# Attention with logits and ranks in PSUM, two chunks' routing interleaved, weight loads behind the chunks, last ranks ahead of the gathered rows

## The chip, the cores and the metric

The kernel runs on one core of one Trainium2 chip, as one launch. The metric is device time in microseconds (us), the median of three runs. The engines are named as in the profile: PE is TensorE (matrix products), PEld its loading of the stationary operand, DVE VectorE, ACT ScalarE, POOL GpSimd, SP SyncE, which only issues transfers. L525 is line 525 of the kernel whose profile or instruction list is shown. PSUM is the accumulator memory behind PE, eight banks of 512 fp32 numbers per partition; SBUF is the on-chip memory of the other operands.

## The reference

Three parts follow each other on 3072 tokens of width 512: a linear attention with a decaying state, a mixture of experts of which each token takes one, and a gated block.

```python
# attention: 4 batches, 8 heads, 768 tokens, head size 64
for t in range(S):
    state = gamma * state + einsum('bhd,bhe->bhde', k[:, :, t], v[:, :, t])
    y[:, :, t] = scale * einsum('bhd,bhde->bhe', q[:, :, t], state)
# mixture: 8 experts, 512 -> 1024 -> 512
logits = x @ w_gate;  e_idx = argmax(logits, axis=1)
gate_w = softmax(logits)[arange(N), e_idx];  eom = sigmoid(x @ w_output_gate)
for e in range(E):
    mask = e_idx == e
    out[mask] = gate_w[mask] * eom[mask, e] * (relu(x[mask] @ w1[e]) @ w2[e])
# gated block: rms norm, two products 512 -> 1536, silu(g) * val, product back to 512
```

## The kernel before

The attention works through 24 chunks of 128 tokens (4 batches of 6). For chunk n PE makes the products of keys and queries (`qk`, L492), which DVE masks by decay (`am`, L499), then in PSUM bank 4 the sum of queries times state (QS, L515, not in the first chunk of a batch, n = 0, 6, 12, 18) and of masked scores times values (PV, L520). DVE scales this sum by `rs` (one slab for each of the six positions in a batch) into `xt` (L525). The state is updated by the product ST (L538) and copied from PSUM to SBUF, half by ACT (L542) and half by DVE (L543). The products of xt with the identity and both gate matrices (`rows`, L549) give in PSUM banks 5 and 6 the token rows and 16 logits in four parts each; DVE adds the parts into `lg` (L554), ACT copies the rows (L557).

Routing of a chunk: a chain of small DVE operations on 128x8 numbers (L564 to L571) finds the largest logit, the expert as a one-hot vector `ohb`, a running count `run_cnt`, and the gate's argument; ACT takes two exponentials (L570, L574). `place` then lets PE count the rank of each token inside its expert (L580 to L582), DVE makes weight and list position (L583 to L590), ACT scales the row and stores it to `xr` (L613, L617), and POOL scatters the token's number into a list in DRAM (L604).

Behind the chunks expert 0 starts on the first 448 tokens of its list. Tokens from older chunks are gathered from `xr` by POOL (L280) and turned by PE (`settle_in`, L629); tokens of the last `NDIRECT` chunks are brought in by a product with a 0/1 matrix `pt` (`direct_in`, L620) of the row's rounded part `rh` and its remainder `rl`. `split` divides the sum in PSUM into two operands, and the expert's products follow (L310, L323).

The expert weights (64 tiles of 128x1024) are loaded by SP (`loads_to`) and split in two by ACT (L179) and POOL (L180) (`convs_to`); the first `NPRE` of them beside the chunks, one tile at every odd n from 3 on. The order of each engine's instructions is the order of the code: in one pass of the loop `load(n+3)`, `vscale(n+1)`, `qk(n+1)`, `rows(n-1)`, `qs_pv(n)`, `st_up(n)`, `place(n-1)`, then weights. A tracker of tiles adds the waits between engines; PSUM is one tile with eight banks for it, and it orders accesses of two engines to the same bank.

Of the kernel before, what the change touches and what calls it, by code (L numbers as in the profile page):

```python
# [103 lines left out]
def fused_kernel(  # L104
# [336 lines left out]
    with ExitStack() as es:  # L441
# [86 lines left out]
        def st_up(n):  # L528
# [13 lines left out]
            ACT.activation(out=s[0:64, :, 0:64], in_=v[0:64], func=AF.Copy)  # L542
            DVE.tensor_copy(out=s[64:128, :, 64:128], in_=v[64:128])  # L543

        def rows(n):
# [14 lines left out]
            sc = tp.tile([128, 12], F32, name="sc", tag="sc")  # L560
            col = [sc[:, i:i + 1] for i in range(12)]
            mx, pm, nmx, sm, nz, ez, s1, t1, gw, pos = col[:10]
            ohb = tp.tile([128, NE], BF16, name="ohb", tag="ohb")
            DVE.tensor_reduce(out=mx, in_=lg[:, 0:8], axis=AX.X, op=ALU.max)  # L564
            DVE.scalar_tensor_tensor(out=junk[:, 0], in0=lg[:, 0:8], scalar=mx, in1=prio, op0=ALU.is_ge, op1=ALU.mult)
            DVE.tensor_scalar(out=nmx, in0=mx, scalar1=-1.0, scalar2=None, op0=ALU.mult)
            DVE.tensor_reduce(out=pm, in_=junk[:, 0], axis=AX.X, op=ALU.max)
            DVE.tensor_scalar(out=ohb, in0=prio, scalar1=pm, scalar2=None, op0=ALU.is_equal)
            DVE.tensor_tensor(out=run_cnt[:, n + 1], in0=run_cnt[:, n], in1=ohb, op=ALU.add)
            ACT.activation(out=junk[:, 1], in_=lg[:, 0:8], func=AF.Exp, bias=nmx, accum_out=sm)  # L570
            DVE.scalar_tensor_tensor(  # L571
                out=junk[:, 2], in0=lg[:, 8:16], scalar=-1.0, in1=ohb, op0=ALU.mult, op1=ALU.mult, accum_out=nz
            )
# [526 lines left out]
```

## Time and profile before

| | us |
|---|---|
| median of three runs (range) | 1115.93 (1115.77 to 1116.07) |
| profiled execution, its own time | 1114.17 |
| its span | 1112.2 |
| PE busy in the span | 1054.8 (95%) |
| DVE busy | 545.0 (49%) |
| ACT busy | 382.3 (34%) |
| POOL busy | 336.0 (30%) |

The span runs from the first to the last recorded instruction; the profiled execution's own time is 2.0 us longer. PE is busy for 95% of the span, but not evenly: in the page's 40 slices of 27.8 us its busy tenths are 7, 7, 8, 8, 7, 8 and then 9 almost to the end. The first five slices hold the chunks, and there DVE stands at 4, 6, 9, 9 and 9 tenths. The chunks end at about 151 us and the first product of expert 0 begins at 171.47 us.

### The profile page before, as it was taken

Reading aid. Unit: us, or ns where it says so; the run is one execution under the profiler, and the core shown is the slowest. Engines: PE = TensorE matmul, PEld = TensorE weight load, DVE = VectorE, ACT = ScalarE, POOL = GpSimd, SP = SyncE. Lnnn points to the kernel's source line nnn. Section 1 sums busy time; section 2 is a strip of 40 time slices with the busy share of each in tenths; the row PEclk is TensorE's granted clock in tenths of the full one; section 3 lists DMA queues with packets and bytes.
Section 4 is the critical chain, followed back from the end, with each engine's and each line's share of the span. In section 5 each row is a group of like instructions: output and inputs, shape, how many; then the busy total and the mean of one; then the engine's idle time right before and its main releaser. Section 6 shows DMA issues by size and latency. Waiting matters only on the chain.

```text
span 1112.2 us, 16373 instructions
## 1 busy us (share of the span) xinstructions
PE 1054.8 (95%) x6393; PEld 985.4 (89%) x6394; DVE 545.0 (49%) x1045; ACT 382.3 (34%) x721; POOL 336.0 (30%) x271
## 2 busy tenths in 40 slices
PE   7788789999999999989899999999999999999995
PEld 6777769989999999988788999999999999999995
DVE  4699953256665676898888731111311122311111
ACT  1344433444444544565555431111311112211111
POOL 3355534556566656432433310000110000200002
PEclk9899989999999999999999999999999999999998
DMA  8999724446446555443343230000200000100001
GB/s 303 254 295 268 213 63 140 124 129 207 153 137 207 183 156 172 155 108 94 111 141 114 86 95 19 1 1 1 85 29 1 1 1 29 57 1 1 1 1 60
DMA packets 47864, 116.74 MB, mean 105 GB/s; under 512 B 12966, under 2 KB 24486, under 8 KB 44962
## 3 DMA queue, kind: packets, MB, share of 16 engines
q1 hardware_dynamic: 39602, 97.05, 28.9%
q0 software_dynamic: 4864, 12.53, 3.2%
q10 hardware_dynamic: 3312, 6.03, 1.5%
q8 instruction: 52, 0.85, 0.3%
q14 instruction: 34, 0.28, 0.1%
HBM read 93.06 MB, written 23.11 MB: 104 GB/s over the span
## 4 chain that ended last, share of the span: by engine, by line
issue 42%; PE 26%; DVE 8%; ACT 4%; POOL 4%; DMA 2%; POOLq 0%; DVEq 0%; ACTq 0%
PE ps L310 12%; PE ps L323 12%; DVE fb L203 2%; POOL out_dram L805 2%; POOL w L180 1%; DVE fb L200 1%; PE ps L296 1%; ACT fu L191 1%; DMA out_dram<-ob,perm 1%; DVE a L780 1%; ACT w L179 1%; DVE fu L206 1%; DVE fb L194 1%; PE ps L629 1%; ACT fu L192 1%
## 5 line engine op out<-in xcount | busy, mean ns | idle before, releaser
L772 PE MATMUL ps<-zh,w 128*128 128x384 f32 x960 | 257.5, 339 | 6.1 <-ACT a L779 6.1
L780 DVE TENSOR_TENSOR a<-a,ps 128x384 f32<-128x384 f32 x96 | 53.0, 552 | 322.7 <-PE ps L772 314.6
L772 PEld LDWEIGHTS ps<-zh,w 128*128 128x128 f32 x960 | 176.6, 190 | 10.9 <-ACT a L779 8.7
L180 POOL TENSOR_TENSOR w<-raw,w 128x1024 fp32r<-128x1024 f32 x64 | 154.7, 2428 | 102.6 <-ACT w L179 101.9
L772 PE MATMUL ps<-zl,w 128*128 128x384 f32 x480 | 162.4, 338 | 0.0
L772 PE MATMUL ps<-xh,w 128*128 128x384 f32 x576 | 154.5, 339 | 4.0 <-DVE a L780 2.6
L310 PE MATMUL ps<-xh,w 128*128 128x448 f32 (+7 forms) x512 | 149.6, 353 | 0.1
L790 PE MATMUL ps<-w,ah 128*128 128x512 f32 x564 | 145.3, 392 | 0.2 <-ACT ys L345 0.2
L805 POOL DMA_INDIRECT out_dram<-xw,perm x10 | 9.9, 992 | 420.9 <-ACT xw L803 417.9
L781 ACT ACTIVATE ah<-a 128x384 fp32r<-128x384 f32 x94 | 49.4, 525 | 203.7 <-DVE a L780 203.7
L790 PEld LDWEIGHTS ps<-w,ah 128*128 128x128 f32 x564 | 104.7, 188 | 16.5 <-ACT ys L345 0.6
L779 ACT ACTIVATE a<-ps 128x384 f32<-128x384 f32 x96 | 46.7, 487 | 200.8 <-PE ps L772 200.8
L772 PEld LDWEIGHTS ps<-xh,w 128*128 128x128 f32 x576 | 104.9, 188 | 7.1 <-DVE a L780 3.3
L323 PE MATMUL ps<-hh,w 128*128 128x448 f32 (+7 forms) x512 | 106.6, 350 | 0.0
L310 PEld LDWEIGHTS ps<-xh,w 128*128 128x128 f32 x512 | 95.2, 188 | 3.5
L772 PE MATMUL ps<-xl,w 128*128 128x384 f32 x288 | 96.9, 337 | 0.0
L323 PEld LDWEIGHTS ps<-hh,w 128*128 128x128 f32 x512 | 93.8, 188 | 2.9
L772 PEld LDWEIGHTS ps<-zl,w 128*128 128x128 f32 x480 | 91.0, 190 | 2.1
L310 PE MATMUL ps<-xl,w 128*128 128x448 f32 (+7 forms) x256 | 89.9, 351 | 0.0
L180 POOL TENSOR_TENSOR w<-fu,w 128x512 fp32r<-128x512 f32 x36 | 54.1, 1504 | 113.3 <-ACT w L179 113.3
L790 PE MATMUL ps<-w,al 128*128 128x512 f32 x282 | 80.1, 392 | 0.0
L782 DVE TENSOR_TENSOR al<-a,ah 128x384 fp32r<-128x384 f32 x94 | 52.5, 559 | 55.6 <-ACT ah L781 55.6
(154 smaller groups left out, 1490.5 us busy)
## 6 DMA issues: line engine op xcount, KB each, us to landing
raw<-wmoe SPq DMA_DIRECT2D x64, 512.0 KB
qkv<-att SPq DMA_DIRECT2D x22, 1024.0 KB
raw<-wm SPq DMA_DIRECT2D x36, 512.0 KB
xw<-z SPq DMA_DIRECT2D x8, 768.0 KB
xr<-row ACTq DMA_DIRECT2D x23, 256.0 KB
z<-ys SPq DMA_DIRECT2D x2, 912.0 KB
z<-ys SPq DMA_DIRECT2D x2, 896.0 KB
z<-ys SPq DMA_DIRECT2D x2, 864.0 KB
```

Source lines behind the costliest of these rows:

```text
L179: ACT.activation(out=dst[:, 0, c], in_=src, func=AF.Copy)
L180: POOL.tensor_tensor(out=dst[:, 1, c], in0=src, in1=f32(dst[:, 0, c]), op=ALU.subtract)
L203: lambda: DVE.scalar_tensor_tensor(out=b, in0=hi, scalar=-(1 << 30), in1=b, op0=ALU.bitwise_and, op1=ALU.bitwise_or),
L310: PE.matmul(p, lhsT=wtile[:, s, k * 128:(k + 1) * 128], rhs=x[w % len(xh)][:, k, 0:n], start=(i == 0), stop=(i == 3 * KB - 1),)
L323: PE.matmul(ps[:, 4 + k, 0:n], lhsT=wtile[:, s, 512 + k * 128:512 + (k + 1) * 128], rhs=h, start=(f == 0 and j == 0), stop=(f == NF - 1 an ...
L772: PE.matmul(ps[:, part, 0:BT], lhsT=w2(f, part, s, k * 128, (k + 1) * 128), rhs=zz[:, k], start=(i == 0), stop=(i == 3 * KB - 1),)
L779: ACT.activation(out=a, in_=ps[:, 0, 0:BT], func=AF.Silu)
L780: DVE.tensor_tensor(out=a, in0=a, in1=ps[:, 1, 0:BT], op=ALU.mult)
L781: ACT.activation(out=ah, in_=a, func=AF.Copy)
L782: DVE.tensor_tensor(out=al, in0=a, in1=f32(ah), op=ALU.subtract)
L790: PE.matmul(ps[:, o_bank[b % 2][t]], lhsT=x[:, t * 128:(t + 1) * 128], rhs=w2(f, 2, s, 0, 512), start=(f == 0 and j == 0), stop=(f == NF2 ...
L805: ins = POOL.indirect_dma_start(out=out[:, :], out_offset=bass.IndirectOffsetOnAxis(ap=pm[:, t0 + t], axis=0), in_=o, in_offset=None, boun ...
```

## The change

Logits: `lg` is no tile in SBUF any more but sixteen columns of PSUM bank 5, beside the rows. The gate matrices are negated once, so that the chain looks for the smallest logit and the negation `nmx` goes. Ranks: they add up in PSUM bank 7 over all chunks, with the products of `ohb` by `rest` (one minus the triangular matrix `uh`) and by `uh`; `run_cnt` goes. Routing: `choose(n-1)` (finding the expert) and `weigh(n-2)` (weight and position) are written as lists and issued one from each in turn; the rank of chunk n-2 stands between PV and ST of chunk n, and `place(n-2)` holds scatter, scaling and store.

State: ACT copies it whole; it is 64 wide rather than 128 with zeros, so QS is eight products with 64 partitions and 64 columns of the stationary operand instead of four with 128. The slabs rs[1] to rs[5] (256 KB each) are no longer loaded but made by ACT from rs[0], four operations in each of the passes n = 0 to 4. Weights: four tiles are asked for in passes 20 to 23, two converted in the loop and two behind it; expert 0's own pass converts the following ones at 1.5 a step from four on, where before it began at eight. `NDIRECT` is 4 instead of 3, so the list is read back after the scatter of chunk 19, and the gather is issued at n = 23 and not at n = 22. The order behind the loop is new.

```diff
-NPRE = 8
+NPRE = 6
...
-NDIRECT = 3
+NDIRECT = 4
...
+        ranks = ps[:, 7, 0:8]
+        lg = ps[:, 5, 320:336]
...
-                    PE.matmul(
-                        o[:, a], lhsT=st_sb[n % 2][:, a], rhs=qT[:, a], start=(a == 0), stop=True, skip_group_check=True
-                    )
+                    for r in (0, 64):
+                        PE.matmul(
+                            o[r:r + 64, a], lhsT=st_sb[n % 2][r:r + 64, a], rhs=qT[r:r + 64, a],
+                            start=(a == 0), stop=True, skip_group_check=True,
+                        )
...
-            ACT.activation(out=s[0:64, :, 0:64], in_=v[0:64], func=AF.Copy)
-            DVE.tensor_copy(out=s[64:128, :, 64:128], in_=v[64:128])
+            ACT.activation(out=s, in_=v, func=AF.Copy)
...
-            lg = tp.tile([128, 16], F32, name="lg", tag="lg")
...
+        def rank(n):
+
+            if n:
+                PE.matmul(ranks, lhsT=rest, rhs=rt[n - 1][2], start=False, stop=True, skip_group_check=True)
+            else:
+                PE.matmul(ranks, lhsT=oh[0:1], rhs=e3[0:1], start=True, stop=True, skip_group_check=True)
+            PE.matmul(ranks, lhsT=uh, rhs=rt[n][2], start=False, stop=True, skip_group_check=True)
...
+            nm, pm, sm, nz, ez = [sc[:, i:i + 1] for i in range(5)]
+
+            def chosen():
+                DVE.tensor_scalar(out=ohb, in0=prio, scalar1=pm, scalar2=None, op0=ALU.is_equal)
+                ACT.activation(out=junk[:, 1], in_=lg[:, 0:8], func=AF.Exp, scale=-1.0, bias=nm, accum_out=sm)
+
+            def gate():
+                DVE.scalar_tensor_tensor(
+                    out=junk[:, 2], in0=lg[:, 8:16], scalar=1.0, in1=ohb, op0=ALU.mult, op1=ALU.mult, accum_out=nz
+                )
+                ACT.activation(out=ez, in_=nz, func=AF.Exp)
...
+                lambda: DVE.tensor_reduce(out=nm, in_=lg[:, 0:8], axis=AX.X, op=ALU.min),
+                lambda: DVE.scalar_tensor_tensor(
+                    out=junk[:, 0], in0=lg[:, 0:8], scalar=nm, in1=prio, op0=ALU.is_le, op1=ALU.mult
+                ),
...
+            ii = tp.tile([128, 1], I32, name="ii", tag="ii", bufs=3)
+            rt[n] = (lg, sc, ohb, gw, pos, ii)
+            return [
+                lambda: DVE.tensor_scalar(out=s1, in0=sm, scalar1=1e-9, scalar2=None, op0=ALU.add),
+                lambda: DVE.scalar_tensor_tensor(
+                    out=junk[:, 3], in0=ranks, scalar=1.0, in1=ohb, op0=ALU.mult, op1=ALU.mult, accum_out=pos
+                ),
+                lambda: DVE.tensor_scalar(out=t1, in0=ez, scalar1=1.0, scalar2=s1, op0=ALU.add, op1=ALU.mult),
+                lambda: DVE.tensor_copy(out=ii, in_=pos),
+                lambda: DVE.reciprocal(out=gw, in_=t1),
...
+        def in_turn(*lists):
+            for i in range(max(len(x) for x in lists)):
+                for x in lists:
+                    if i < len(x):
+                        x[i]()
...
-            rk = ps[:, 7, (n % 2) * 8:(n % 2) * 8 + 8]
-            PE.matmul(rk, lhsT=oh[0:1], rhs=e3[0:1], start=True, stop=False)
-            PE.matmul(rk, lhsT=oh, rhs=run_cnt[:, n], start=False, stop=False)
-            PE.matmul(rk, lhsT=uh, rhs=ohb, start=False, stop=True)
...
-            if 2 <= n + 2 < CPB:
-                SP.dma_start(out=rs[:, n + 2], in_=rsc[:, n + 2])
...
-            if n == NCH - 2:
+            if n == NCH - 1:
                 ex.gather(0, CAPS[0], NT - NDIRECT * CH)
             qk(n + 1)
             if n >= 1:
                 rows(n - 1)
             qs_pv(n)
+            if n >= 2:
+                rank(n - 2)
             st_up(n)
-            if 1 <= n < NCH - 1:
-                place(n - 1)
-            if n == NCH - 3:
+            if n + 1 < CPB:
+                for a in range(NP):
+                    g = A_GROW + n * NP + a
+                    ACT.activation(out=rs[:, n + 1, a], in_=rs[:, 0, a], func=AF.Copy, scale=ca[:, g:g + 1])
+            in_turn(choose(n - 1) if n >= 1 else [], weigh(n - 2) if n >= 2 else [])
+            if n >= 2:
+                place(n - 2)
+            if n == NCH - NDIRECT + 1:
                 ex.load_list(0, CAPS[0], 0)
-            if n >= 3 and n % 2 == 1:
-                convs_to((n - 3) // 2)
-                loads_to((n - 3) // 2 + 2)
-        direct_in(NCH - 3, True)
+            if n >= NCH - 4:
+                loads_to(n - NCH + 5)
+                if n < NCH - 1:
+                    convs_to(n - NCH + 4)
+        rows(NCH - 1)
+        direct_in(NCH - 4, True)
+        rank(NCH - 2)
+        in_turn(choose(NCH - 1), weigh(NCH - 2))
+        direct_in(NCH - 3, False)
+        rank(NCH - 1)
         place(NCH - 2)
-        rows(NCH - 1)
-        settle_in((0, 1))
+        in_turn(weigh(NCH - 1))
         place(NCH - 1)
-        settle_in((2, 3))
         direct_in(NCH - 2, False)
-        direct_in(NCH - 1, False)
+        convs_to(4)
+        last = CAPS[0] // 128 * 128
+        settle_in(range(0, last, 128))
         for k in range(KB):
+            settle_in(range(last, CAPS[0], 128), (k,))
+            direct_in(NCH - 1, False, (k,))
             ex.split(0, k, CAPS[0], ps[:, k, 0:CAPS[0]])
-        store_row(NCH - 1, *row_t[NCH - 1])
-        convs_to(NPRE)
+        store_row(NCH - 2)
+        store_row(NCH - 1)
...
-            convs_to(min(t + NSLOT - 3, NPRE + max(0, t - 1) * 3 // 2))
+            convs_to(min(t + NSLOT - 3, 4 + t * 3 // 2))
```

The lists below show the order of the instructions on an engine; a name in square brackets is a semaphore on which the instruction waits, and says which engine or transfer queue signals it. On PE, one pass in the middle of the chunk loop, before:

```order
L492 MATMUL ps<-qkv 128x128 [waits DMAHW1_49]
L492 MATMUL ps<-qkv 128x128 x7
L549 MATMUL ps<-iwt,xt 128x144 [waits DVE_49,Activation_49]
...
L515 MATMUL ps<-qkv,st_133 128x128 [waits DVE_49]
L515 MATMUL ps<-qkv,st_133 128x128 x3
L520 MATMUL ps<-am_1233,vt 64x128 [waits Pool_49]
...
L538 MATMUL ps<-vt,qkv 64x64 x8
...
L580 MATMUL ps<-e_129,oh 128x8 [waits DVE_49]
...
L581 MATMUL ps<-run_cnt,oh 128x8
...
L582 MATMUL ps<-ohb,uh 128x8 [waits DVE_49]
```

And the same pass now:

```order
L495 MATMUL ps<-qkv 128x128 [waits DMAHW2_49]
L495 MATMUL ps<-qkv 128x128 [waits DVE_49]
...
L553 MATMUL ps<-iwt,xt 128x144 [waits DVE_49]
...
L519 MATMUL ps<-qkv,st_133 64x128 x8
L525 MATMUL ps<-am_1399,vt 64x128 [waits Pool_49]
...
L571 LDWEIGHTS rest
L571 MATMUL ps<-ohb,rest 128x8
...
L574 MATMUL ps<-ohb,uh 128x8
L543 MATMUL ps<-vt,qkv 64x64 x8
```

QS has eight products, the rank moved ahead of ST, and `rows` waits for DVE alone, while the wait of QS for DVE's half of the state is gone; the products of the rank wait for nothing. On DVE, from the sum of the logits of one chunk to the routing, before:

```order
L554 TENSOR_REDUCE lg<-ps 128x16 [waits PE_49]
L564 TENSOR_REDUCE sc<-lg 128x1 [waits DVE_49]
L565 SCALAR_TENSOR_TENSOR junk<-lg,sc,ca 128x8 [waits DVE_49]
L566 TENSOR_SCALAR sc<-sc 128x1
L567 TENSOR_REDUCE sc<-junk 128x1 [waits DVE_49]
L568 TENSOR_SCALAR ohb<-ca,sc 128x8 [waits DVE_49]
L569 TENSOR_TENSOR run_cnt<-run_cnt,ohb 128x8 [waits DVE_49]
L571 SCALAR_TENSOR_TENSOR junk,sc<-lg,ohb 128x8
L525 TENSOR_TENSOR xt<-ps,rs 128x512 [waits PE_49]
L543 COPY st_134<-ps 64x4x64 [waits Activation_49]
L583 TENSOR_SCALAR sc<-sc 128x1
...
L585 SCALAR_TENSOR_TENSOR junk,sc<-ps,ohb 128x8 [waits PE_49]
```

And now (L591 to L585 are `choose` of one chunk, L606 to L612 `weigh` of the chunk ahead of it):

```order
L558 TENSOR_REDUCE ps<-ps 128x16 [waits DVE_49,PE_49]
L530 TENSOR_TENSOR xt<-ps,rs 128x512 [waits PE_49]
L591 TENSOR_REDUCE sc<-ps 128x1 [waits Activation_49]
L606 TENSOR_SCALAR sc<-sc 128x1
L592 SCALAR_TENSOR_TENSOR junk<-ps,sc,ca 128x8 [waits DVE_49]
L607 SCALAR_TENSOR_TENSOR junk,sc<-ps,ohb 128x8 [waits PE_49]
L595 TENSOR_REDUCE sc<-junk 128x1 [waits DVE_49]
L610 TENSOR_SCALAR sc<-sc 128x1
L581 TENSOR_SCALAR ohb<-ca,sc 128x8 [waits DVE_49]
L611 CAST ii<-sc 128x1 [waits DMASW2_49]
L585 SCALAR_TENSOR_TENSOR junk,sc<-ps,ohb 128x8 [waits DVE_49,Activation_49]
L612 RECIPROCAL sc<-sc 128x1
```

`xt` (L525, now L530) stands ahead of the whole chain and no longer behind it, the copy of the state has left DVE, and the reduction L591 waits for ACT, whose copy of the rows is in the same bank. On PE behind the loop, before, with the direct rows L620, the gathered rows L629 (each of the four waits is for one part of the gather) and the first product of the expert L310:

```order
L620 MATMUL ps<-pt,rh 128x448 [waits DVE_49,Activation_49]
...
L582 MATMUL ps<-ohb,uh 128x8 [waits DVE_49]
L549 MATMUL ps<-iwt,xt 128x144 [waits DVE_49,Activation_49]
...
L629 MATMUL ps<-cs,xw 128x128 [waits DMASW5_49]
L629 MATMUL ps<-cs,xw 128x128 [waits DMASW6_49]
L629 MATMUL ps<-cs,xw 128x128 [waits DMASW7_49]
L629 MATMUL ps<-cs,xw 128x64 [waits DMASW0_49]
...
L582 MATMUL ps<-ohb,uh 128x8 [waits DVE_49]
L629 MATMUL ps<-cs,xw 128x128 x3
...
L620 MATMUL ps<-pt,rh 128x448 [waits Activation_49]
...
L620 MATMUL ps<-pt,rh 128x448 [waits DVE_49,Activation_49]
...
L310 MATMUL ps<-xh_99,w_87 128x448 [waits DVE_49]
```

And now, where these lines are L651, L660 and L311:

```order
L553 MATMUL ps<-iwt,xt 128x144 [waits DVE_49]
...
L651 MATMUL ps<-pt,rh 128x448
...
L574 MATMUL ps<-ohb,uh 128x8
L651 MATMUL ps<-pt,rh 128x448 [waits DVE_49,Activation_49]
...
L574 MATMUL ps<-ohb,uh 128x8 [waits DVE_49]
L651 MATMUL ps<-pt,rh 128x448 [waits DVE_49,Activation_49]
...
L660 MATMUL ps<-cs,xw 128x128 [waits DMASW5_49]
...
L660 MATMUL ps<-cs,xw 128x128 [waits DMASW6_49]
...
L660 MATMUL ps<-cs,xw 128x128 [waits DMASW7_49]
...
L660 MATMUL ps<-cs,xw 128x64 [waits DMASW0_49]
L651 MATMUL ps<-pt,rh 128x448 [waits DVE_49,Activation_49]
...
L311 MATMUL ps<-xh_97,w_87 128x448 [waits DVE_49]
```

All direct rows but those of chunk 23 and all rank products now stand ahead of the gathered rows; the last part of these alternates with the direct rows of chunk 23, column block by column block.

## Rows read from the trace of the kernel before

**Rows 1.** Stretches of one core: busy us of each engine, granted clock, DMA.

```profile
21.63:151.05 129.42, 108.68 (x1390) 98.37 (x1385) 113.78 (x414) 53.62 (x135) 63.14 (x71) 0.96 0.83 237
151.05:171.47 20.42, 16.72 (x69) 13.55 (x67) 6.32 (x30) 5.31 (x14) 7.24 (x10) 0.67 0.20 58
171.47:240.00 68.53, 68.53 (x342) 62.85 (x343) 25.63 (x52) 28.50 (x43) 39.44 (x21) 1.00 0.46 145
```

**Rows 2.** Timeline of VectorE, chunk 1: start us, us, engine, line, operation.

```profile
21.63 0.69 DVE L525 TENSOR_TENSOR xt<-ps,rs 128x512 f32<-128x512 f32 x1 [0.50 <-PE ps L520]
```

**Rows 3.** Waits in the chunk loop: us in total, times, longest us.

```profile
ACT row L557 <- DVE lg L554: 12.1, 8, 5.6
...
PE ps L492 <- DMA qkv<-att: 6.0, 2, 4.4
```

**Rows 4.** Timeline of TensorE over chunk 22, start us, us.

```profile
141.22 1.16 PE L492 MATMUL ps<-qkv 64*128 64x128 f32 x16
142.31 1.25 PE L549 MATMUL ps<-iwt,xt 128*128 128x144 f32 x8
143.39 1.05 PE L515 MATMUL ps<-qkv,st 128*128 128x128 f32 x8
144.38 1.09 PE L520 MATMUL ps<-am,vt 128*64 128x128 f32 x16
145.30 0.63 PE L538 MATMUL ps<-vt,qkv 128*64 128x64 f32 x16
...
147.17 0.36 PE L549 MATMUL ps<-iwt,xt 128*128 128x144 f32 x1 [0.81 <-DVE xt L525]
```

**Rows 5.** Timeline of VectorE, the routing of chunk 22 while GpSimd computes nothing.

```profile
149.96 0.16 DVE L564 TENSOR_REDUCE sc<-lg 128x1 f32<-128x8 f32 x1
150.16 0.23 DVE L565 SCALAR_TENSOR_TENSOR junk<-lg,sc,ca 128x8 f32<-128x8 f32 x1
...
150.62 0.23 DVE L568 TENSOR_SCALAR ohb<-ca,sc 128x8 bf16<-128x8 f32 x1
...
150.96 0.16 DVE L571 SCALAR_TENSOR_TENSOR junk<-lg,ohb 128x8 f32<-128x8 f32 x1
...
151.05 0.69 DVE L525 TENSOR_TENSOR xt<-ps,rs 128x512 f32<-128x512 f32 x1
```

**Rows 6.** VectorE in the loop by line: count, busy us, mean ns, idle before.

```profile
L569 DVE TENSOR_TENSOR run_cnt<-run_cnt,ohb 128x8 bf16<-128x8 bf16 x22 | 13.0, 593 | 0.8
L565 DVE SCALAR_TENSOR_TENSOR junk<-lg,sc,ca 128x8 f32<-128x8 f32 x22 | 12.9, 584 | 0.8
...
L585 DVE SCALAR_TENSOR_TENSOR junk<-ps,ohb 128x8 f32<-128x8 f32 x22 | 3.6, 165 | 0.6
```

**Rows 7.** Timeline of all engines at a weight conversion inside the loop.

```profile
86.93 2.37 POOL L180 TENSOR_TENSOR w<-raw,w 128x1024 fp32r<-128x1024 f32 x1 [0.91 <-ACT w L179]
87.01 2.32 DVE L571 SCALAR_TENSOR_TENSOR junk<-lg,ohb 128x8 f32<-128x8 f32 x1
```

**Rows 8.** ScalarE in the loop by line.

```profile
L542 ACT ACTIVATE st<-ps 64x256 f32<-64x256 f32 x19 | 6.9, 361 | 0.7 <-PE ps L538 0.7
L570 ACT ACTIVATE junk<-lg,sc 128x8 f32<-128x8 f32 x21 | 6.2, 298 | 6.9 <-DVE sc L566 6.9
...
L570 ACT ACTIVATION_READ_ACCUMULATOR junk<-lg,sc 128x1 f32 x21 | 3.9, 188 | 0.0
```

**Rows 9.** Timeline of all engines behind the loop: GpSimd, then TensorE.

```profile
143.52 1.01 POOL L604 DMA_INDIRECT lst<-ids,ii  x1 [2.95 <-DVE ii L590]
...
151.75 1.07 POOL L280 DMA_INDIRECT xw<-xr,ix  x1 [6.12 <-issue]
```

**Rows 10.** Timeline of TensorE: gathered rows and direct rows.

```profile
162.13 4.44 PE L629 MATMUL ps<-cs,xw 128*128 128x128 f32 x16
...
170.02 0.36 PE L620 MATMUL ps<-pt,rh 128*128 128x448 f32 x1
170.22 0.37 PE L620 MATMUL ps<-pt,rl 128*128 128x448 f32 x1
```

More of the change, by code (lines that the diff above doesn't have):

```diff
@@ L451, in fused_kernel @@
         uh = ap.tile([128, 128], BF16, name="uh")
+        rest = ap.tile([128, 128], BF16, name="rest")
         oh = ap.tile([128, 128], BF16, name="oh")
@@ L456, in fused_kernel @@
         slots = ap.tile([128, CAPS[0]], F32, name="slots")
-        st_sb = [ap.tile([128, NP, 128], F32, name=f"st{i}") for i in range(2)]
-        run_cnt = ap.tile([128, NCH + 1, NE], BF16, name="run_cnt")
+        st_sb = [ap.tile([128, NP, D], F32, name=f"st{i}") for i in range(2)]
         junk = ap.tile([128, 4, NE], F32, name="junk")
@@ L559, in rows @@
             )
[L560 to L573, printed above, removed]
@@ new lines, in choose @@
+        def choose(n):
+            lg, sc, ohb = rt[n]
+            nm, pm, sm, nz, ez = [sc[:, i:i + 1] for i in range(5)]
[12 more added lines that the diff above has]
+                ),
+                lambda: DVE.tensor_reduce(out=pm, in_=junk[:, 0], axis=AX.X, op=ALU.max),
+                chosen,
+                gate,
+            ]
@@ new lines, in weigh @@
+        def weigh(n):
+            lg, sc, ohb = rt[n]
+            sm, nz, ez, s1, t1, gw, pos = [sc[:, i:i + 1] for i in range(2, 9)]
+            ii = tp.tile([128, 1], I32, name="ii", tag="ii", bufs=3)
+            rt[n] = (lg, sc, ohb, gw, pos, ii)
+            return [
+                lambda: DVE.tensor_scalar(out=s1, in0=sm, scalar1=1e-9, scalar2=None, op0=ALU.add),
[5 more added lines that the diff above has]
+                lambda: DVE.reciprocal(out=gw, in_=t1),
+            ]
@@ L634, in totals_a @@
         def totals_a():
-            PE.matmul(ps[:, 7, 32:40], lhsT=oh, rhs=run_cnt[:, NCH], start=True, stop=True)
+            PE.matmul(ranks, lhsT=rest, rhs=rt[NCH - 1][2], start=False, stop=True, skip_group_check=True)
         def totals_b():
             cnt = ap.tile([1, 1, 8], F32, name="cnt")
-            DVE.tensor_copy(out=cnt, in_=ps[0:1, 7, 32:40].rearrange("p (o e) -> p o e", o=1))
+            DVE.tensor_tensor(
+                out=cnt, in0=ranks[0:1].rearrange("p (o e) -> p o e", o=1),
+                in1=ca[0:1, A_E3:A_E3 + 8].rearrange("p (o e) -> p o e", o=1), op=ALU.subtract,
+            )
             s3 = [1, 8, 8]
@@ L682, in fused_kernel @@
         SP.dma_start(out=cs, in_=cst)
-        SP.dma_start(out=rs[:, 1], in_=rsc[:, 1])
         DVE.tensor_copy(out=uh, in_=ca[:, A_U:A_U + 128])
+        DVE.tensor_scalar(out=rest, in0=ca[:, A_U:A_U + 128], scalar1=-1.0, scalar2=1.0, op0=ALU.mult, op1=ALU.add)
         DVE.memset(oh, 1.0)
@@ L688, in fused_kernel @@
         DVE.tensor_copy(out=ids, in_=ca[:, A_IDS:A_IDS + NCH])
-        DVE.memset(run_cnt[:, 0], 0.0)
+        gates = iwt[:, :, 128:144]
+        DVE.tensor_scalar(out=gates, in0=gates, scalar1=-1.0, scalar2=None, op0=ALU.mult)
         fill = {
```

71 lines of the change are left out of this document (31 added, 40 removed).

## The prediction, made before the changed kernel ran

> **What bounds the kernel now.** I read the stretches first. From the `xt` of chunk 1 at 21.63 us [rows 2] to that of chunk 23 at 151.05 us, 22 steps take 129.42 us, 5.88 each; PE is busy for 108.68 of them and DVE for 113.78, the clock is 0.96. From there to the first product of expert 0 it is 20.42 us, PE busy 16.72 at a mean clock of 0.67. From 171.47 us on PE is busy in all of 68.53 us out of 68.53 [rows 1]. So the change can gain in the first two stretches and only lose in the third.
>
> Which engine holds a step is read from the timelines. On PE chunk 22 goes: QK 141.22, rows 142.31, QS 143.39, PV 144.38 (lasting 1.09), ST 145.30 (0.63), so by starts 1.09, 1.08, 0.99, 0.92 and 0.57; with 0.16 for the ranks, the two small products that remain, 4.81 us of work. The next `rows` starts only at 147.17 behind a wait of 0.81 for `xt` [rows 4]. On DVE that `xt` stands behind the routing. Where POOL computes nothing the chain from L564 at 149.96 to the end of L571 at 151.12 takes 1.16 us and `xt` starts inside its tail, at 151.05, and takes 0.69 [rows 5]. Where POOL converts a weight tile (L180, 2.37 us from 86.93) the 0.16 us operation L571 beside it takes 2.32 [rows 7]. Over the loop L565 has a mean of 584 ns and L569 of 593, against 0.23 and 0.16 to 0.23 for such operations in the quiet stretch, while L585, which reads PSUM, has 165 [rows 5, 6]. These stalls, ahead of `xt`, make the steps long. Besides, PE waits for the loads of qkv for 6.0 us, in two places [rows 3].
>
> **The change part by part.** First the loop. Conversions leave it up to pass 20, and with them the 2.3 us stalls; `run_cnt` (L569) goes; the loads of rs (5 times 256 KB) and of weights leave the queue, so I also take the 6.0 us as gone. What is late next is not PE alone. The order on DVE is now `lg`, `xt`, then choose and weigh in turn; and as `lg` lies in bank 5, `rows` of the next chunk waits for the last operation of choose that reads it, the gate's (L585). That is a ring: `rows` 1.08, QS 0.99, PV 1.09 to its end, 0.05 to DVE, `xt` 0.69, the ten operations 1.17 (the eight of the quiet chain took 1.16 with their gaps; the five of weigh stand in gaps that the others need for their results), 0.1 back to PE: 5.17 us [rows 4, 5]. The 0.05 and 0.1 are my estimates of a signal, from gaps of this size between the rows of that timeline. PE's other work in the ring's second half, ranks, ST and QK (0.16 + 0.57 + 1.09 = 1.82), fits beside its 2.01. So a step costs 5.17, and a chunk with c = 0 (6, 12, 18), which has no QS, 4.18.
>
> In passes 1 to 4 ACT makes the next slab of rs. The exponential of the chosen logit stands behind these four operations and the state's copy on ACT, and the gate's operation waits for it since both read bank 5. From PV's start: 0.92 + 0.16 + 0.63 to the end of ST (1.71), 0.05, the copy 0.36, four times 0.30, 0.05, the exponential 0.30 and its read 0.19, 0.05, the gate 0.24, 0.1; with `rows` and QS 6.32 us [rows 4, 5, 8]. The 0.30 for 128 columns has no row: its bounds are 0.19 and 0.36 (256 columns), and I take the value of the exponential's row, the middle one. That puts a step between 5.9 and 6.6.
>
> Sum of the loop: 15 x 5.17 + 3 x 4.18 + 4 x 6.32 = 77.6 + 12.5 + 25.3 = 115.4 us against 129.4: 14.0 less. QS in eight products is costed at its old 0.99: 64 partitions and 64 columns each, in two quarters of the array that can work at once. Its price has no row; below it could be nothing less, above it is twice 0.99 if they take turns. The nearest row is PV, eight products of 64 columns on 128 partitions, 0.92 [rows 4], and I stay with 0.99. The state's whole copy by ACT (0.36, [rows 8]) ends beside QK, and DVE loses its half, which stood behind `xt`. Scatter and scaling come one pass later; POOL and ACT are busy for 63.14 and 53.62 of 129.42 [rows 1], which covers them.
>
> Second, the stretch behind the loop. From `xt` of chunk 23: `xt`, routing and signal 2.0, `rows` 1.08, then direct rows of chunks 20, 21 and 22, 24 passes at 0.20 (170.02 to 170.22, full clock, [rows 10]) 4.8, ranks 0.3. The last of these waits for chunk 22's remainder `rl`, which follows the rank, position and scaling of that chunk; I put 0.8 on it, with bounds of 0 and 2. The gathered rows: eight products took 4.44 at half clock [rows 10], so sixteen take 4.4 at full. Direct rows of chunk 23 1.6, split to the first product 0.25. Together 15.2 against 20.4: 5.2 less. The gather was issued 8.2 us after the scatter of its last chunk (143.52 to 151.75, [rows 9]); now its last chunk is 19, scattered in pass 21, and the gather is issued behind the conversion in pass 22, about 2 us after the start of this stretch. With four pieces it ends before the PE wants the first, some 8 us in; so it costs nothing, and a miss by 2 us would.
>
> Third, expert 0 starts with four tiles converted rather than eight. POOL is busy for 39.44 of 68.53 us there [rows 1], so 29.1 are free, and four more conversions at 2.37 [rows 7] are 9.5. Step t needs tile t, and the schedule is at least three tiles ahead from the start, so I cost it at nothing; without that cover it would be up to 9.5.
>
> Sum: 1114.17 - 14.0 - 5.2 = 1095.0 for a profiled execution. The median stood 1.76 above the profiled one, so I predict 1096.7 us.
>
> **The rivals.** A, the ring doesn't hold: `rows` does not wait for choose, or DVE's ten operations are done in less, and PE alone is the bound. Then 15 x 4.81 + 3 x 3.82 + 4 x 4.81 = 102.9 in the loop, 12.5 less, so 1084.2. For it: ACT's row copy and DVE's sum L554 read the same bank, and the tracker could know columns. Against it: that row copy waited for L554 for 12.1 us in 8 places [rows 3], though both only read, so order goes by bank. Of such sharing the Trainium skill ("PSUM — Partial Sum Buffer", "PSUM bank collisions raise a hardware error") says that software must keep two engines from the same part of a bank at once, even two readers or at different columns. By that rule the ring stays, and by it alone A would be nothing; that row of the copy agrees. I keep 12% for A, because only one pair of engines shows it.
>
> B, the slower side: the eight QS products take turns instead of running in pairs, and PE stops at the changes of tile shape, which now stand ahead of and behind QS. Turns cost 0.99 in each of 19 chunks, 18.8 us; changes at most 0.2 each, two in 22 chunks, 8.8 (the gap between the starts of QS and PV leaves no more unexplained, [rows 4]). That is 1096.7 + 27.6 = 1124.3. It decides the sign from a QS of about 2.0 us on, since 19.2 us over 19 chunks is 1.01 each. For it: each product has half the rows and half the columns of the array, and twice as many are issued. Against it: ST too is made of 64-column products, and its sixteen passes take 0.63 [rows 4]. The Trainium skill ("TensorEngine Tiling (Array Packing)", "Key Properties") says that tiles may work at the same time but that a change of tiling drains the engine, which would speak for the second half of B. The trace has a change of shape from QK to rows (64 to 128 partitions), and there rows start 1.09 after a QK of 1.16, without a gap [rows 4].
>
> C, the clock: the stretch behind the loop ran at a mean of 0.67, 1.2 GHz for most of it, after PE's waits [rows 1]. PE still waits 2.0 us there for `xt` and routing. If the clock falls as before, 0.33 x 20.42 = 6.7 us come back: 1103.4.
>
> D, the moved conversions: expert 0 waits for its tiles, up to 9.5 us: 1106.2. For it: ACT and DVE also split and scale there, and DVE stalls while POOL converts [rows 7]. Against it: POOL's 29.1 free us [rows 1].
>
> **How the numbers follow.** Forecast 60%, A 12%, B 8%, C 8%, D 8%, the rest 4%. The forecast's own range is 1088 to 1103: the rs steps give 1.7 less to 1.1 more, the tail 0.8 less to 2 more, and 0.2 a step either way in 18 steps 3.6. Toward A and D I take 1083 to 1109, which leaves out B and the ends of the rest. A measurement of this kernel can tell a change of about 0.2%, 2.2 us. Faster than that are the forecast, A, C, D and part of the rest, 0.90; within it and slower come from B and from mishaps that add up, 0.04 and 0.06.
>
> **What the profile would show.** The ring: `rows` waiting for DVE's gate operation, about 0.2 us of PE idle a step, starts of `xt` 5.17 apart and longer by 1.1 in passes 1 to 4. Starts 4.8 apart would be A. QS longer than 1.05 would be B. The stretch behind the loop at a clock near 1 and 15 us long; a clock of 0.67 is C. Waits of expert 0's products for `w` are D. If no wait for qkv is left but the steps stay at 5.9, the stalls of DVE were not what held them, and the forecast is wrong in its first step.

## The result, and the profile after

| | before | changed |
|---|---|---|
| median of four executions each (range) | 1115.85 (1113.57 to 1116.07) | 1104.99 (1100.29 to 1105.03) |
| median on another chip, eleven and five executions (e16) | 1117.51 | 1108.43 |
| span of the profiled execution among the first four | 1112.2 | 1098.6 |

The ratio is 0.9887 with a 95% interval of 0.9871 to 0.9902, and 0.9919 (0.9902 to 0.9935) on the other chip. So it is 10.9 us faster, where 19.2 was forecast. 1104.99 lies inside the range of 1083 to 1109 and above the forecast's own 1088 to 1103. One execution of e13 below took 1187.68 us at a granted clock of 0.844, where all others have 0.977 or more; it is left out of e13's median.

Stretches of the changed kernel, in the columns of [rows 1]: from `xt` of chunk 1 to that of chunk 23, from there to the first product of expert 0, and a first part of the expert:

```profile
19.51:136.66 117.15, 106.83 (x1512) 90.61 (x1508) 71.79 (x346) 49.78 (x145) 45.98 (x63) 1.00 0.86 227
136.66:157.54 20.88, 15.77 (x80) 12.75 (x78) 9.74 (x41) 9.46 (x18) 15.58 (x15) 0.84 0.50 138
157.54:228.50 70.96, 70.72 (x355) 64.16 (x355) 27.65 (x52) 34.21 (x50) 49.51 (x25) 1.00 0.55 168
```

The first stretch falls from 129.42 to 117.15 us, 12.3 less, with DVE busy for 71.79 us instead of 113.78. The second is 20.88 against 20.42, although its granted clock is 0.84 instead of 0.67. Chunk 1's `xt` starts 2.1 us earlier than in [rows 2], and the rest, from the first product of the expert to the end, is 941.1 against 940.7. These four make the 13.6 us between the two spans. In two further traces of the changed kernel (e16 and e1) chunk 1's `xt` starts at 21.96 and 21.81 us, so the 2.1 us are not shown to be the change's. The loop takes 119.73 and 122.51 us there, so its gain over the one trace of the kernel before is 6.9 to 12.3 us, where 14.0 was forecast.

One step of the loop on DVE (start us, us), to set beside [rows 5]:

```profile
84.00 0.69 DVE L530 TENSOR_TENSOR xt<-ps,rs 128x512 f32<-128x512 f32 x1 [1.82 <-PE ps L525]
...
85.25 0.23 DVE L581 TENSOR_SCALAR ohb<-ca,sc 128x8 bf16<-128x8 f32 x1
...
85.59 0.17 DVE L585 SCALAR_TENSOR_TENSOR junk<-ps,ohb 128x8 f32<-128x8 f32 x1
...
89.16 0.69 DVE L530 TENSOR_TENSOR xt<-ps,rs 128x512 f32<-128x512 f32 x1 [1.82 <-PE ps L525]
```

And on PE, to set beside [rows 4]:

```profile
84.63 1.16 PE L495 MATMUL ps<-qkv 64*128 64x128 f32 x16
85.82 1.25 PE L553 MATMUL ps<-iwt,xt 128*128 128x144 f32 x8
87.00 1.09 PE L519 MATMUL ps<-qkv,st 64*64 64x128 f32 x16
88.02 1.09 PE L525 MATMUL ps<-am,vt 128*64 128x128 f32 x16
89.04 0.18 PE L571 MATMUL ps<-ohb,rest 128*128 128x8 bf16 x1
...
89.18 0.69 PE L543 MATMUL ps<-vt,qkv 128*64 128x64 f32 x16
89.79 0.38 PE L495 MATMUL ps<-qkv 64*128 64x128 f32 x2
```

`xt` starts 5.16 us apart. The gate's operation L585 ends at 85.76 and `rows` begins at 85.82, while QK began at 84.63. At two of the added changes of shape the starts lie further apart: rows to QS is 1.18 where it was 1.08, PV to rank 1.02 where PV to ST was 0.92 (the rank also changes from fp32 to bf16, and no run separates the two). What PE waited for in the loop, to set beside [rows 3] (us in total, times, longest us):

```profile
PE ps L553 <- DVE junk L585: 7.0, 8, 1.3
PE ps L495 <- DMA qkv<-att: 3.1, 5, 1.2
```

And DVE's operations with SBUF operands, to set beside [rows 6]:

```profile
L581 DVE TENSOR_SCALAR ohb<-ca,sc 128x8 bf16<-128x8 f32 x22 | 5.3, 243 | 0.0
...
L592 DVE SCALAR_TENSOR_TENSOR junk<-ps,sc,ca 128x8 f32<-128x8 f32 x22 | 5.0, 226 | 0.0
```

L581, which reads SBUF alone, has 243 ns, where L565 and L569 had near 600. L592 reads its logits from PSUM and has 226.

### The profile page after: what moved, and what is told of

Same layout as the page of the kernel before. It is cut to its first block, busy times and chain, and to the rows that moved or that the text cites. A ratio compares the mean times of both kernels' runs of the same rounds, so it can differ in the third digit from the quotient of the medians.

```text
span 1098.6 us, 16579 instructions
## 1 busy us (share of the span) xinstructions
PE 1049.3 (96%) x6537; PEld 973.3 (89%) x6538; DVE 505.8 (46%) x980; ACT 387.9 (35%) x742; POOL 336.7 (31%) x269
## 4 chain that ended last, share of the span: by engine, by line
issue 40%; PE 37%; DVE 9%; ACT 4%; DMA 4%; POOL 3%; SPq 1%; POOLq 0%; DVEq 0%
PE ps L311 12%; PE ps L324 11%; DMA qkv<-att 3%; PE ps L818 3%; DVE fb L204 2%; PE ps L553 2%; POOL out_dram L851 2%; PE ps L525 2%; PE ps L519 1%; POOL w L181 1%; DVE fb L201 1%; PE ps L297 1%; PE ps L836 1%; PE ps L495 1%; ACT fu L192 1%
## 5 line engine op out<-in xcount | busy, mean ns | idle before, releaser
L311 PE MATMUL ps<-xh,w 128*128 128x448 f32 (+7 forms) x512 | 149.7, 354 | 0.0
L311 PEld LDWEIGHTS ps<-xh,w 128*128 128x128 f32 x512 | 95.3, 188 | 3.2
L311 PE MATMUL ps<-xl,w 128*128 128x448 f32 (+7 forms) x256 | 90.0, 351 | 0.0
```

Source lines behind the costliest of these rows:

```text
L311: PE.matmul(p, lhsT=wtile[:, s, k * 128:(k + 1) * 128], rhs=x[w % len(xh)][:, k, 0:n], start=(i == 0), stop=(i == 3 * KB - 1),)
```

## The experiments

They were measured in three groups, each on a chip of its own beside runs of the kernel before (medians 1117.96, 1118.04 and 1117.51 us). A trace is split into the loop (`xt` of chunk 1 to that of chunk 23), the stretch behind it (to the first product of expert 0) and the rest. Beside them stand PE's waits for qkv and the granted clock in the loop. All times are in us; "one" marks a single execution.

| run | group | loop | waits for qkv | clock | behind | rest | median |
|---|---|---|---|---|---|---|---|
| changed | first | 117.2 | 3.1 | 1.00 | 20.9 | 941.1 | 1104.99 |
| e1_again | 1 | 122.5 | 5.0 | 0.97 | 19.4 | 941.2 | 1106.68 (one) |
| e2_loads_first | 1 | 125.3 | 8.1 | 0.97 | 19.4 | 941.0 | 1109.60 |
| e3_lg_sbuf | 1 | 119.6 | 10.1 | 0.96 | 21.5 | 941.5 | 1104.51 |
| e5_rs_late | 1 | 123.4 | 7.0 | 0.96 | 23.0 | 941.2 | 1106.77 |
| e4_conv_behind | 2 | 121.4 | 6.2 | 0.99 | 17.5 | 945.2 | 1108.90 |
| e7_noload | 2 | 106.0 | 0 | 1.00 | 21.9 | 943.4 | 1094.05 (one) |
| e8_noload_ring | 2 | 115.4 | 0 | 1.00 | 24.5 | 941.1 | 1105.60 (one) |
| e9_weights_in_loop | 2 | 127.4 | 9.4 | 0.97 | 16.6 | 941.0 | 1108.13 |
| e16_after_timed | 3 | 119.7 | 5.4 | 1.00 | 22.4 | 941.1 | 1108.43 |
| e13_q5 | 3 | 120.5 | 4.5 | 0.99 | 18.2 | 941.1 | 1102.77 |
| e15_all | 3 | 122.6 | 6.2 | 0.96 | 17.1 | 942.9 | 1106.97 |
| e14_all_q5 | 3 | 112.1 | 0 | 1.00 | 17.2 | 943.2 | 1099.80 |

**e1_again and e16_after_timed**, the changed kernel without an edit. 

> The changed kernel once more, for a second trace: of its four executions the profiled one took 1100.29 us and the others 1105.0. Theory 1: the 4.7 us lie behind the loop, in how long TensorE stays at 1.2 GHz after its wait of 4.8 us for the gate operation of chunk 22; the loop is then 117.2 us from the xt of chunk 1 to that of chunk 23, as in the first trace, and the stretch to expert 0 is 25 us instead of 20.9. Theory 2: they lie in the loop, in waits of QK for qkv, 3.1 us in the first trace; the loop is then up to 122.

> The changed kernel once more, timed beside the three versions of this call on the same chip. If its times differ from chip to chip by the waits for qkv, as the two traces say, it takes 1105 to 1108 us here; the stretch behind the loop is 19 to 21 us, with rows(22) waiting 3 to 5 us.

PE's waits in the loop of e1_again:

```profile
PE ps L553 <- DVE junk L585: 7.4, 7, 2.0
PE ps L495 <- DMA qkv<-att: 5.0, 4, 2.2
```

The loop is 5.4 us longer than in the first trace, the stretch behind it 1.5 shorter. So theory 2 is right on where the time lies, for this trace, and in part on why. The waits for qkv are 1.9 us more; PE is also busy for 3.0 us more, at a lower clock (0.97 over the loop). The steps with the largest waits for loads take 8.9 and 6.5 us instead of 5.2. The last step takes 7.6 without such a wait. There L581 takes 1.12 us beside GpSimd's conversion and the operation behind that, `rows` waits 2.0 us for the gate after it, and the clock over the step is 0.78. Against the first trace this step is 2.2 of the 5.4 us. For the three executions that took 1105.0 there is no trace, so for them none of this is shown.

In e16 `rows` waited 7.0 us behind the loop, where 3 to 5 were expected, and the stretch is 22.4 us, not 19 to 21. Its median, 1108.43, lies just above the 1105 to 1108.

**e8_noload_ring.** In `load`:

```diff
...
+                if n > 3:
+                    a_t[n] = first[n % 4]
+                    return
...
```

> Chunks 4 to 23 use the q, k and v of the first four chunks again instead of loading their own, so the output is another one; all else is the changed kernel. Theory 1 (what the loop takes above the sum by the ring, 115.4 us, are waits of QK for its loads: 117.2 us in the first trace, 122.5 in the second): the loop takes 114 to 116 us, steps of 5.16 and no step above 6.4. Rival (long steps come from something else, a scatter or a store that others wait for): the loop stays at 117 to 123 us with single steps of 8 to 10.

The loop takes 115.35 us, and PE's only wait in it is the ring's:

```profile
PE ps L557 <- DVE junk L589: 8.0, 8, 2.0
```

Theory 1 holds: without loads the sum by the ring, 115.4, is met to 0.1 us. That closeness is in part luck: the four steps with rs take 24.4 us where the sum had 25.3, and the last step, in which L581 is held for 1.12 us, takes 6.05 where it had 5.17. What the loop takes above 115.4 in other runs hangs on loads, apart from e1's last step. Behind the loop it is 24.5 us here, with ScalarE waiting 6.6 for the load of tile 1, the wait that e2 takes away.

**e7_noload.** The same, and in `rows`

```diff
...
-        lg = ps[:, 5, 320:336]
...
+            lg = tp.tile([128, 16], F32, name="lg", tag="lg", bufs=3)
...
```

> As the run without loads (chunks 4 to 23 use the first four chunks' data), and the logits in an SBUF tile as well. Theory 1 (with neither ring nor loads TensorE's own work is left, 5.06 us a step as seen with the logits in SBUF, and not 4.81): steps of 5.06, 3.4 without QS, the loop 106 to 109 us. Rival (5.06 was set by the transfers): steps of 4.8 to 4.9 and a loop of 101 to 104.

PE over a step, now without a wait:

```profile
84.47 1.16 PE L498 MATMUL ps<-qkv 64*128 64x128 f32 x16
85.56 1.25 PE L556 MATMUL ps<-iwt,xt 128*128 128x144 f32 x8
86.74 1.09 PE L522 MATMUL ps<-qkv,st 64*64 64x128 f32 x16
87.76 1.09 PE L528 MATMUL ps<-am,vt 128*64 128x128 f32 x16
88.79 0.18 PE L574 MATMUL ps<-ohb,rest 128*128 128x8 bf16 x1
...
88.92 0.69 PE L546 MATMUL ps<-vt,qkv 128*64 128x64 f32 x16
89.54 1.16 PE L498 MATMUL ps<-qkv 64*128 64x128 f32 x16
```

Theory 1 holds: 5.07 from QK to QK, the loop 106.0 us, of which PE is busy 105.6. PE's own work is 5.06, not the 4.81 of rival A; 0.10 each stands at rows to QS and PV to rank.

**e3_lg_sbuf.** The logits edit alone. 

> The logits are put in an SBUF tile again; all else is as in the changed kernel. Theory 1 (a step of 5.17 us is the ring rows, QS, PV, xt, choose, closed by bank 5; TensorE's work is next): steps of 4.8 to 4.9 us in 15 passes, some 5 us off the loop, 1099 to 1100. Rival (the transfers are next: the DMA engines are 0.96 busy at 249 GB/s between 48 and 130 us, 1.31 MB a step): steps of 5.05 to 5.15 with waits of QK for qkv in their place, 1103 to 1105. Rival 2 (operations with two SBUF operands stall beside GpSimd again, as in the kernel before): steps above 5.2.

The ring goes, the steps are 5.06, and waits for qkv of 10.1 us come in; the time is the first rival's, 1104.51. Its reason is half right: the waits are there, but they act at single steps, and the 5.06 is PE's own, as e7 shows it without any loads. Rival 2 did not come: L592 and L581 (L591 and L580 in this kernel), the first now with both inputs in SBUF, have means of 268 and 254 ns. Only one conversion lies in the loop here.

**e5_rs_late.** The loop over `a` with the operations for rs stands behind this line and not ahead of it:

```diff
...
+            in_turn(choose(n - 1) if n >= 1 else [], weigh(n - 2) if n >= 2 else [])
...
```

> ScalarE's four operations for the next slab of rs stand behind the routing of the chunk and not ahead of its exponential. Theory 1 (in passes 1 to 4 the exponential waits behind them, and the gate and the next rows wait for it): the steps 2 to 5, 5.8 to 6.3 us now, fall to 5.2, 3.5 to 4 us less in the loop, 1101 to 1102. Rival (transfers set these steps, since the first loads and the fills stand there): the wait moves to QK for qkv, and the loop gains less than 1 us.

Steps 2 to 5 are 5.31, 5.24, 5.24 and 5.23 against 5.79, 6.28, 6.14 and 6.15 in e1_again, 3.3 less. But two waits for loads, 7.0 us, follow, and the loop is no shorter than e1's. This trace is of the longest of its four executions (1113.27 us), but the median is e1's time as well. Both are right: theory 1 in the mechanism, and the rival in what is gained.

**e9_weights_in_loop.**

```diff
-            if n >= NCH - 4:
-                loads_to(n - NCH + 5)
-                if n < NCH - 1:
-                    convs_to(n - NCH + 4)
+            if n >= 3 and n % 2 == 1:
+                convs_to(min((n - 3) // 2, 4))
+                loads_to(min((n - 3) // 2 + 2, 4))
```

> The four weight tiles are asked for and converted in the loop again, at odd passes from 3 on. Theory 1 (conversions beside the routing stall VectorE's operations with two SBUF operands, of which only ohb is left, and so lengthen a step by up to 2.3 us each): four steps longer by 1 to 2.3 us, the loop 4 to 8 us above that of the changed kernel (117 to 122.5), the stretch behind it shorter by the 3 to 5 us that rows(22) waited there; in sum within 4 us of the changed kernel. Rival (the loads matter, 2 MB in the busy part of the queue at some 250 GB/s, 8 us): the waits of QK for qkv grow by 4 us or more, and the kernel is slower than the changed one by over 4 us.

The loop is 127.4 us, 5 to 8 above e1 and e16; the stretch behind it 16.6, 2.8 to 5.8 less; the median is theirs. That is theory 1's sum, but largely by the rival's means: the waits for qkv are 9.4 us, and L581 is held at two of the four conversions only (1.15 and 1.13 us).

**e2_loads_first.** Ahead of `ex.load_list`:

```diff
+            if n == NCH - 3:
+                loads_to(3)
```

> The requests for weight tiles 1 and 2 stand ahead of the reading of the list on SyncE. Theory 1 (the list's wait for its scatter held tile 1's load from 117 to 133.9 us; ScalarE then stood at that tile's conversion, and with it the row copy, choose and rows(22)): no wait of ScalarE for raw, rows(22) starts as soon as the ring allows, about 0.5 us after the gate, the stretch behind the loop falls from 20.9 us to 15 to 17, and the median from 1105.0 to 1099 to 1101. Rival (the stretch is long because the clock fell after the loop's end in any case): ScalarE's wait goes, the stretch stays above 19, the median above 1103.

ScalarE's wait for raw (the buffer that a weight tile is loaded into) is gone, and the stretch is 19.4 us, as in e1. GpSimd, DVE and PE behind the loop:

```profile
148.16 2.34 POOL L181 TENSOR_TENSOR w<-raw,w 128x1024 fp32r<-128x1024 f32 x1
148.24 0.23 DVE L592 SCALAR_TENSOR_TENSOR junk<-ps,sc,ca 128x8 f32<-128x8 f32 x1
...
148.70 1.85 DVE L581 TENSOR_SCALAR ohb<-ca,sc 128x8 bf16<-128x8 f32 x1
...
150.89 2.29 PE L553 MATMUL ps<-iwt,xt 128*128 128x144 f32 x8 [3.36 <-DVE junk L585]
```

The conversion begins 0.5 us ahead of L581 and holds it for 1.85 us, and `rows` waits 3.36. L592, which starts inside the same conversion with its logits from PSUM, is not held. So the number is the rival's, and the reason another: when ScalarE's wait went, GpSimd's hold took its place. e4 was made to take that away as well.

**e4_conv_behind.** Tile 3 is loaded over tile 0 ahead of its conversion here, so expert 0 computes with tile 3's data in both places.

```diff
-                if n < NCH - 1:
-                    convs_to(n - NCH + 4)
```

> The two weight conversions that stand in passes 21 and 22 go behind the loop, with the other two. Theory 1 (with the loads moved ahead, rows(22) still waited 3.4 us, since GpSimd's conversion of tile 1 then stalled VectorE's ohb, 1.85 us, beside it; so the conversion itself has to go): rows(22) waits under 1 us, the clock stays at 1.0 behind the loop, the stretch from the xt of chunk 23 to expert 0 falls from 19.4 to 21 us to 15 to 16.5, and expert 0 waits for no tile. Rival (expert 0 waits, since its first tile is converted only about 14 us into the stretch): the stretch is no shorter than 18 us, its last wait that of the first product for w.

The stretch is 17.5 us, `rows` waits 1.7. Then PE waits in the expert:

```profile
PE ps L324 <- ACT hh L317: 2.2, 1, 2.2
PE ps L553 <- DVE junk L585: 1.7, 1, 1.7
```

Neither wait is as expected: `rows` was to wait under 1 us, and the rival's last wait was for a tile. It is not its tile that is late but hh, the expert's first result, which ACT copies from PSUM. ACT itself waits there, for the stores of the last two rows (L645):

```profile
167.57 0.54 ACT L317 ACTIVATE hh<-ps 128x448 fp32r<-128x448 f32 x1 [4.82 <-DMA xr<-row]
```

In the changed kernel ACT has this wait too, 2.2 us long, and PE none behind it. GpSimd's conversions also hold DVE's totals (L683 1.59 and L686 2.36 us), but hh does not wait for these: in e7 they take 0.15 and 0.21 us, and ACT waits 4.5 us for the same stores. Why the stores are late is open. The rest is 4.1 longer. I had costed conversions beside expert 0's start at nothing; with all four there 4 us are lost, by a wait that neither side named, and that the conversions cause it is not shown.

**e13_q5, e15_all and e14_all_q5.** e13 has the first three lines, e15 the last with the edits of e2 and e5, e14 all of them.

```diff
...
+        qp = pool(es, "qkv", 5)
...
+        load(3)
...
+            load(n + 4)
...
+                if n < NCH - 2:
...
```

> Three moves at once: weight tiles 1 and 2 asked for ahead of the list, the conversion of tile 1 behind the loop (that of tile 0 stays in pass 21), the operations for rs behind the routing. Theory 1: the stretch behind the loop 16.5 to 17.5 us instead of 19 to 21, passes 1 to 4 shorter by 3.5 us together as far as loads allow; 2 to 6 us below the changed kernel beside it. Rival (the waits for loads and for the conversions behind the loop take it back, as when each was tried alone): within 2 us of it.

> Five buffers for q, k and v instead of four, each load issued one pass earlier; all else is the changed kernel. Theory 1 (the loads come late because a load can start only when a buffer is free, while the queue idles at times: DMA busy share 0.83 to 0.86 over the loop): the waits of QK for qkv fall under 2 us, the loop to 115 to 117 us, 4 to 6 us less than the changed kernel beside it. Rival (the transfer engines give no more while stores and scatters run beside the loads): the waits stay at 4 us or more and the time within 2 us.

> The three moves and five buffers for q, k and v. Theory 1 (both bounds were separate: loads in the loop, the conversions behind it): the loop 112 to 114 us, the stretch behind it 16.5 to 17.5, 7 to 11 us below the changed kernel beside it. Rival (transfers bound the loop whatever the buffers): no more than the version without the fifth buffer gains.

e15 without the fifth buffer gains 1.5 us over e16, with ranges that overlap: its rival. Passes 1 to 4 and the stretch behind the loop get shorter as theory 1 says, but the waits for qkv are 6.2 us and the clock is 0.96. e13 gains 5.7. Its median is theory 1's, but its trace does not show theory 1's reason: the waits for qkv still sum to 4.5, the loop is no shorter than e16's, and the gain lies behind the loop (18.2 us against 22.4), where `rows` waits 2.9 us and not 7.0. e14 gains 8.6, as its theory 1 says, with a ratio to before of 0.9845 (0.9829 to 0.9861). Its loop and the stretch behind it:

```profile
22.93:135.01 112.08, 106.73 (x1512) 90.61 (x1508) 72.55 (x346) 50.74 (x146) 45.77 (x62) 1.00 0.91 234
135.01:152.18 17.17, 14.94 (x80) 11.94 (x78) 9.01 (x41) 8.92 (x18) 13.28 (x15) 0.90 0.53 100
```

PE does not wait for qkv once. By the medians the fifth buffer is worth 7.2 us with the other three edits (e14 against e15) and 5.7 without them; that it is worth more when the steps are short is not shown. e14 is faster than both kernels, as the highest of its five times, 1100.78, is below the changed kernel's lowest on that chip, 1106.80.

## Why the prediction was right, and where it was not

**The ring: right.** 5.17 a step was predicted, 5.16 measured; 4.18 without QS, 4.14; 115.4 for the loop, 115.35 without loads. The mechanism is shown: PE waits for L585, and with the logits out of the bank (e3, e7) the step is 5.06. That the step agrees to 0.01 is luck: rows and QS take 0.13 more than in the sum, and choose, with the signals, 0.14 less. In passes 1 to 4 I had 6.32 and the trace has 5.78, 6.29, 6.14 and 6.14. One of these on all engines:

```profile
38.47 0.39 ACT L547 ACTIVATE st<-ps 128x256 f32<-128x256 f32 x1 [1.94 <-PE ps L543]
...
38.75 1.26 ACT L747 ACTIVATE rs<-rs,ca 128x128 f32<-128x128 f32 x4
...
39.92 0.25 ACT L582 ACTIVATE junk<-ps,sc 128x8 f32<-128x8 f32 x1
...
40.29 0.17 DVE L585 SCALAR_TENSOR_TENSOR junk<-ps,ohb 128x8 f32<-128x8 f32 x1 [1.03 <-ACT junk L582]
...
40.52 1.25 PE L553 MATMUL ps<-iwt,xt 128*128 128x144 f32 x8 [1.00 <-DVE junk L585]
```

The four operations take 1.26 us (I had 1.20), the exponential starts behind them, the gate behind its read, and `rows` behind the gate: the chain as it was written down.

**DVE's stalls: right.** DVE is busy for 42 us less. Of these 24.3 are three operations that are gone: `run_cnt` (L569, 13.0, its own stalls with it), DVE's half of the state's copy (8.1) and the negation (3.2). L565, L568 and L571 fell from 28.0 to 14.0 (now L592, L581 and L585). That the stalls made the steps long shows in single steps of the kernel before, which their mean of 5.88 hides:

```profile
94.31 0.69 DVE L525 TENSOR_TENSOR xt<-ps,rs 128x512 f32<-128x512 f32 x1
...
98.57 2.33 DVE L569 TENSOR_TENSOR run_cnt<-run_cnt,ohb 128x8 bf16<-128x8 bf16 x1
...
100.91 0.68 DVE L525 TENSOR_TENSOR xt<-ps,rs 128x512 f32<-128x512 f32 x1
...
105.97 0.69 DVE L525 TENSOR_TENSOR xt<-ps,rs 128x512 f32<-128x512 f32 x1
```

A step with a conversion takes 6.60 us, the next without one 5.06. Of the 22 steps eleven take 5.05 to 5.07, all without a conversion; the eight with one take 5.95 to 7.58, or 10.27 where a load is late too. So the loop's gain lies in the steps that had a conversion or a late load. The ordinary step did not get shorter: it went from 5.06 to the ring's 5.16, and e3 has 5.06 again. Which part of the change keeps the stalls small is not separated: they stay small with the logits in SBUF and no conversions but one (e3), and for L592 with the logits in PSUM and four conversions (226 ns in e9).

Where GpSimd's work still stands beside L581, it is held: 1.27 us behind the loop in the first trace, 1.85 in e2. The Trainium skill ("SBUF — State Buffer", "SBUF: two separate sides") says that a VectorE operation with two SBUF inputs, or in a mode with two ports, and one of GpSimd hold a shared port pair for whole instructions, one after the other. The traces agree: L581 is held until the conversion ends (which of the two kinds it is, no run shows), and L592 in e2, with its logits in PSUM, takes 0.23 us inside the same conversion.

**Rival A fell twice.** The ring holds, and PE alone is 5.06. The Trainium skill ("TensorEngine Tiling (Array Packing)", "Key Properties") says that a change of tiling drains TensorE; here the starts lie 0.10 us further apart at two of the added changes. That is half of the 0.2 that I took as rival B's bound. QS itself costs 1.02 against 0.99: the tile pairs do run together, and B did not come.

**"I also take the 6.0 us as gone": wrong.** I took the loads of rs and weights off the queue and with them all waits for qkv. They are 3.1 us in the first trace, 5.0 and 5.4 in e1 and e16. I asked what leaves the queue, and not what a shorter step asks of it: 1 MB of loads and 256 KB of stores now come every 5.17 us and not every 5.88. That this is why waits are left is argued, not shown: over the loop the transfers ran at 227 GB/s, no more than the 237 before.

**The stretch behind the loop, 15.2 us: wrong by 5.7.** I wrote 2.0 us from `xt` to `rows`; it is 4.89. What was held, on all engines:

```profile
132.86 0.38 SPq L274 DMA_DIRECT2D ix<-lst  x1
...
133.93 7.60 SPq L184 DMA_DIRECT2D raw<-wmoe  x4
...
137.71 1.06 ACT L180 ACTIVATE w<-raw 128x1024 fp32r<-128x1024 f32 x1 [2.05 <-DMA raw<-wmoe]
138.67 0.58 ACT L561 ACTIVATE row<-ps 128x512 f32<-128x512 f32 x1
138.85 2.33 POOL L181 TENSOR_TENSOR w<-raw,w 128x1024 fp32r<-128x1024 f32 x1 [1.37 <-ACT w L180]
139.28 0.17 DVE L591 TENSOR_REDUCE sc<-ps 128x1 f32<-128x8 f32 x1 [1.93 <-ACT row L561]
...
139.94 1.27 DVE L581 TENSOR_SCALAR ohb<-ca,sc 128x8 bf16<-128x8 f32 x1
...
141.32 0.17 DVE L585 SCALAR_TENSOR_TENSOR junk<-ps,ohb 128x8 f32<-128x8 f32 x1
...
141.55 2.29 PE L553 MATMUL ps<-iwt,xt 128*128 128x144 f32 x8 [4.79 <-DVE junk L585]
```

SyncE reads the list (L274) only after the scatter of chunk 19, for which it waits 15.5 us, and the requests for the next weight tiles (L184) are queued behind it. So ACT stands 2.05 us at the conversion of tile 1 (L180), chunk 22's row copy (L561) comes after it, choose (L591) after the copy because of their bank, and GpSimd's half of the conversion then holds L581 for 1.27. `rows` waits 4.79 us. I had looked at that conversion for what it does to the gather and to expert 0, and not at who is queued behind it on ACT. Behind PE's wait the clock is at its lower level, 1.2 GHz (the columns are those of [rows 1]):

```profile
141.50:147.00 5.50, 5.45 (x19) 4.78 (x20) 1.91 (x8) 2.49 (x6) 4.28 (x5) 0.52 0.88 172
```

At 0.52 these 5.5 us lose 2.6. That and 2.9 for the wait are 5.5 of the 5.7. So rival C came, but for 2.6 of its 6.7 us and by a wait that I did not see. e2, e4 and e9 show the two holds apart; without either the stretch is 16.6 and 17.5 us (e9, e4), still above 15.2.

**Expert 0 with four tiles: right as it stands** (the rest is 0.3 us longer), but near its edge: in e15, e14, e7 and e4 the rest is 1.8 to 4.1 us longer than in the first trace, and in each PE waits 1.5 to 2.2 us for hh, which ACT makes only after the stores of the last rows.

**The sum of the miss.** 1104.99 is 8.3 above 1096.7: 5.7 behind the loop, 1.8 in it, 0.3 in the rest, 2.1 less ahead of it and 0.3 less around the span; the remaining 2.9 are that the three unprofiled executions took 4.7 more than the profiled one, where I had added 1.76. Where those lie stays open. That 1104.99 lies inside 1083 to 1109 is luck rather than foresight: the room was taken toward A and D, and neither came. The forecast's own range is also wider than its terms: 1.7, 0.8 and 3.6 less give 1090.6, not 1088.

## What to carry to other kernels

Read steps one by one before taking their mean: here a mean of 5.88 was a mix of steps of 5.06 and steps of 6 to 10. An instruction that waits for a transfer holds all that is queued behind it on its engine (2.05 us at ACT's conversion became part of 4.79 on PE), and the request for that transfer is itself queued behind the waits of its own queue: follow both before a load is moved. When a loop is made shorter, look at the buffers ahead of its loads; one more was worth 5.7 and 7.2 us here. A ring of dependencies can be summed by hand from durations and starts: the step came out within 0.1 us here, with single terms off by up to 0.1.
